# Sparse attention woven into a gated FFN: a half's scores in two units of six PSUM banks instead of three units of four

## The chip, the cores and the metric

The kernel runs on one core of a Trainium2 chip. Times are device microseconds of one execution. The engines are named as the profile names them: PE is TensorE's matmul stream and PEld its weight loads, DVE is VectorE, ACT is ScalarE, POOL is GpSimd, SP is the engine that issues most of the DMAs.

## The reference

Four sequences of 768 positions, 8 heads of 64 channels. Attention is sparse: a query sees the first 8 keys (global) and the last 96 keys up to itself (local), with a bias that falls with distance. The result is the input of a gated FFN of width 1536.

```python
scores = scale * np.matmul(q, k.transpose(0, 1, 3, 2))
keep = is_global | is_local
scores = np.where(keep, scores + bias, -1e9)
a = softmax(scores)
x = np.matmul(a, v)                      # to 3072 tokens x 512
out = (np.maximum(x @ w_gate, 0.0) * (x @ w_val)) @ w_out
```

## The kernel before

**Halves.** The work is cut into 8 halves of a sequence, 384 queries each (s or c = 0 to 7). Halves 0 and 1 form a start of their own. From then on the FFN of half c runs together with the attention of half c+1, in one stream of instructions: `weave` takes the FFN's pieces in order and puts the attention's pieces between them at given fractions of the stage. `spread(items, first, last, n)` gives piece i the fraction first + (i + 0.5)/n x (last - first). The stages with attention in them are c=1 (FFN of halves 0 and 1, attention of half 2) and c=2 to 6 (attention of halves 3 to 7); c=7 is FFN alone. Even c carries the attention of an odd half, odd c that of an even half, and c=3, 5 and 7 also have seven pieces more of the output product.

**FFN pieces.** For each of 12 column blocks a gate product (`gate`, L748, four matmuls of 384 columns), its Relu on ScalarE (L757), a value product (`val`, L748) and its multiply on VectorE (L764). Then the output product in seven pieces (L634, matmuls of 256 columns), in a form with fewer multiplications that needs sums of activations: `Pair.sums`, L627 to L630 on VectorE, four of which are issued after value products 7 to 10. All products take their PSUM bank from a pool of three, `ff_ps` (FFB).

**Attention pieces of a half.** The scores (`score_unit`, L515) of a pair of head pairs pp, key group g and head e of a pair fill one bank: 12 banks in a half. The contraction is 64 rows, so the matmuls of e=0 and e=1 stand in the two halves of TensorE's rows[...]. An even half has groups of 432, 432 and 336 columns, an odd one of 480, 480 and 432. Each bank gets one exponential on ScalarE (`unit_exp`, L524) and one or two mask multiplies on VectorE (`mask`, L536), which carry bias and mask. A mask is not issued with its exponential but with the next one (or with `flush`, which AV calls first). Then for each head pair p: AV products for the two heads (`piece_av`, L431, bank pool `av_ps` of two, AVB), logarithm (L440) and inverse (L446) of the softmax sum on ScalarE, and the normalization (`piece_norm`, N, L453, two multiplies on VectorE), which frees the two AV banks and writes `xT`, the FFN's input.

**Scores before.** There are three units of two groups, so of four banks: one from AVB, three from the score pool `qk_ps` (QKB, three banks). A half's order is

```python
(X(U[0]) + X() + X() + X() + wait + X(U[1]) + X() + X() + a0[0:1] + X() + a0[1:2] + N(0) + wait
 + X(U[2]) + X() + a1[0:1] + X() + X() + a1[1:2] + N(1) + wait * 2 + AV(2) + N(2) + wait * 2
 + AV(3) + [(0.0, lambda: piece_inverse(s, 3))] + N(3))
```

where X(U) is a unit of scores and its first exponential, X() a further exponential with the mask of the one before, a0 and a1 the AV products of p=0 and 1, and `wait` an empty place. Each engine executes its instructions in the order of this stream.

**Beside it.** GpSimd casts the queries and keys of the half after next and puts the keys in order (`early_pieces`: L367, then L278 to L284), in c=2 to 5. In c=1 VectorE also makes eight sums of the output weights (L600).

Of the kernel before, what the change touches and what calls it, by code (L numbers as in the profile page):

```python
# [8 lines left out]
FP32 = mybir.dt.float32  # L9
# [7 lines left out]
def kernel(  # L17
# [12 lines left out]
    nc = tc.nc  # L30
# [8 lines left out]
    HP = H // 2  # L39
    QH = S // 2  # L40
    NN = 3
# [45 lines left out]
    kT = [[const.tile([128, NT, 128], BF16, name=f"kT{i}_{p}") for p in range(HP)] for i in range(2)]  # L87
# [163 lines left out]
    QKB, FFB, AVB = (qk_psum, "qk_ps"), (ff_psum, "ff_ps"), (av_psum, "av_ps")  # L251
# [114 lines left out]
    def piece_cast2(s, p, dst, src):  # L366
        nc.gpsimd.tensor_copy(  # L367
            dst[s % 2].rearrange("t n (h d) -> t h n d", d=D)[:, 2 * p : 2 * p + 2],
            src[s][:, 2 * p : 2 * p + 2, :].rearrange("t e (n d) -> t e n d", n=NN))

    def piece_x(dst, src, n):
        nc.sync.dma_start_transpose(out=dst[:, :, n * 128 : (n + 1) * 128], in_=src[:, n])

    def piece_order(s, p):
        b, half = divmod(s, 2)
        put_keys(nc.gpsimd.tensor_copy, nc.gpsimd.tensor_copy, kT[b % 2][p], kNb[s % 2][:, p], half)

    def early_pieces(s):
        out = [(0.0, lambda p=p: piece_cast2(s, p, kc, ks_of)) for p in range(HP)]
        out += [(0.0, lambda n=n: piece_x(kNb[s % 2], kc[s % 2], n)) for n in range(NN)]  # L380
        out += [(0.0, lambda p=p: piece_cast2(s, p, qc, qs_of)) for p in range(HP)]
        out += [(0.0, lambda n=n: piece_x(qT2[s % 2], qc[s % 2], n)) for n in range(NN)]
        out += [(0.0, lambda p=p: piece_order(s, p)) for p in range(HP)]
        return out
# [35 lines left out]
    def piece_av(s, p, e):  # L420
        b, half = divmod(s, 2)
        h = 2 * p + e
        vb = vbuf[b % 2]
        av = av_psum.tile([128, 512], FP32, name="av_ps")
        av_of[s, p, e] = av
        av3 = av[:, 0:QH].rearrange("d (n p) -> d n p", n=NN)
        todo = [t for bank in banks_of_half[half] for t in bank]
        for i, (j, a, w, m) in enumerate(todo):
            es, c = es_of[s, p, j, e]
            z0 = 2 * D * h + (D if e == 0 else 0)  # L430
            nc.tensor.matmul(av3[:, :, a : a + w],  # L431
                             lhsT=vb[:, j, z0 : z0 + 128],
                             rhs=es[:, c : c + NN * w].rearrange("k (n p) -> k n p", n=NN),
                             start=(i == 0), stop=(i == len(todo) - 1),
                             skip_group_check=True)
        o0, d0 = (0, 64) if e == 0 else (64, 0)
        if e == 0:
            av_of[s, p, "l"] = rc_pool.tile([128, QH], FP32, name="lnd")
        ln = av_of[s, p, "l"]
        nc.scalar.activation(ln[o0 : o0 + 64], av[d0 : d0 + 64, 0:QH], AF.Ln, bias=0.0, scale=1.0)  # L440
        if e == 1 and p < HP - 1:
            piece_inverse(s, p)

    def piece_inverse(s, p):
        rc = rc_pool.tile([128, QH], FP32, name="rcp")
        nc.scalar.activation(rc, av_of[s, p, "l"], AF.Exp, bias=0.0, scale=-1.0)  # L446
        av_of[s, p, "r"] = rc

    def piece_norm(s, p, e):
        if s not in xT_of:  # L450
            xT_of[s] = xt_pool.tile([128, N_DC, QH], BF16, name="xT")
        r = slice(64 * e, 64 * e + 64)
        nc.vector.tensor_tensor(xT_of[s][r, p, :], av_of[s, p, e][r, 0:QH], av_of[s, p, "r"][r],  # L453
                                op=ALU.mult)
# [20 lines left out]
    def piece_norm_wide(s, p):  # L475
        piece_sums_wide(s, p)
        piece_mul_wide(s, p)
# [17 lines left out]
            xT_of[s] = xt_pool.tile([128, N_DC, QH], BF16, name="xT")  # L495
        nc.vector.tensor_tensor(xT_of[s][:, p, :], av_of[s, p][1][:, 0:QH], av_of[s, p, "r"], op=ALU.mult)

    def score_unit(s, groups, pools):


        b, half = divmod(s, 2)
        out = []
        for pp, g in groups:
            banks = []
            for e in range(2):
                pool, name = pools.pop(0)
                banks.append(pool.tile([128, 512], FP32, name=name))
                out.append((pp, g, e, banks[e]))
            c = 0
            for j, a, w, m in banks_of_half[half][g]:  # L510
                for p in (2 * pp, 2 * pp + 1):
                    for e in range(2):
                        r = slice(64 * e, 64 * e + 64)
                        q3 = qT2[s % 2][r, p].rearrange("d (n p) -> d n p", n=NN)
                        nc.tensor.matmul(banks[e][:, c : c + NN * w], lhsT=kT[b % 2][p][r, j, :],  # L515
                                         rhs=q3[:, :, a : a + w], start=True, stop=True)
                    c += NN * w
        return out

    def unit_exp(s, pp, g, e, ps):  # L520
        bank = banks_of_half[s % 2][g]
        cols = sum(2 * NN * w for _, _, w, _ in bank)
        es = es_pool.tile([128, 480], BF16, name="es")
        nc.scalar.activation(es[:, 0:cols], ps[:, 0:cols], AF.Exp, bias=0.0, scale=scale)  # L524

        def mask():
            c = 0
            for j, a, w, m in bank:
                n_ = 2 * NN * w
                e4 = es[:, c : c + n_].rearrange("k (i n p) -> k i n p", i=2, n=NN)  # L530
                h0 = 4 * pp + e
                mk = m_all[:, h0 : h0 + 3 : 2, 0 if j == 0 else 1, :, m : m + w]
                if w == WQ:
                    e4 = e4.rearrange("k i n p -> k i (n p)")
                    mk = mk.rearrange("k i n p -> k i (n p)")
                nc.vector.tensor_mul(e4, e4, mk)  # L536
                for i in range(2):
                    es_of[s, 2 * pp + i, j, e] = (es, c + i * NN * w)
                c += n_

        return mask

    def attention_pieces(s):
        masks, units = [], []

        def flush():
            for f in masks:
                f()
            masks.clear()

        def scores(groups, pools):
            units.extend(score_unit(s, groups, list(pools)))

        def x(scored=None):
            ready = masks[:]
            masks.clear()
            if scored:
                scores(*scored)
            masks.append(unit_exp(s, *units.pop(0)))
            for f in ready:  # L560
                f()

        U = [([(0, 0), (0, 1)], (AVB, QKB, QKB, QKB)),
             ([(0, 2), (1, 0)], (AVB, QKB, QKB, QKB)),
             ([(1, 1), (1, 2)], (AVB, QKB, QKB, QKB))]
        X = lambda u=None: [(0.0, lambda: x(u))]
        AV = lambda p: [(0.0, lambda e=e: (flush(), piece_av(s, p, e))) for e in range(2)]
        N = lambda p: [(0.0, lambda: (piece_norm(s, p, 0), piece_norm(s, p, 1)))]
        wait = [(0.0, lambda: None)]
        a0, a1 = AV(0), AV(1)  # L570

        return (X(U[0]) + X() + X() + X() + wait + X(U[1]) + X() + X() + a0[0:1] + X() + a0[1:2] + N(0) + wait
                + X(U[2]) + X() + a1[0:1] + X() + X() + a1[1:2] + N(1) + wait * 2 + AV(2) + N(2) + wait * 2
                + AV(3) + [(0.0, lambda: piece_inverse(s, 3))] + N(3))


    out_v = out.rearrange("(s p n) d -> s n p d", p=128, n=NN)

# [229 lines left out]
    def spread(items, first, last, n=None):  # L808

        n = n or len(items)  # L810
        return [(first + (i + 0.5) / n * (last - first), f) for i, (_, f) in enumerate(items)]
# [28 lines left out]
    def AV(s, p, *pools):  # L840
        piece_av_wide(s, p, *pools)
        piece_norm_wide(s, p)
# [139 lines left out]
    def T2_piece(p):  # L982
# [9 lines left out]
          spread(T2, 0.55, 0.95))  # L992
    sums_wo = [(0.0, f) for i in (0, 3) for f in weight_sums(i, i + 3)]
    weave(f1_0[G[2]] + f1_1[G[2]] + f2_0 + f2_1,
          spread(attention_pieces(2), 0.02, 0.86, 30), spread(early_pieces(3), 0.1, 0.76),
          spread(sums_wo, 0.08, 0.4))

    for c in range(2, NHALF):
        placed = []
        if c + 1 < NHALF:  # L1000
            placed.append(spread(attention_pieces(c + 1), 0.0, 0.85 if c % 2 else 0.87, 30))
        if c + 2 < NHALF:
            load_qk(c + 2, 0, H)
            load_v_half(c + 2)
            placed.append(spread(early_pieces(c + 2), 0.25, 0.75))
        f1, f2 = ffn_pieces(c)
        weave(f1 + f2, *placed)
# [35 lines left out]
```

The softmax here doesn't subtract the row's maximum and nothing guards it: scores larger than these inputs give would overflow.

## Time and profile before

Three runs: median 238.47 us, from 237.69 to 238.80. The profiled execution has a span of 235.6 us.

| engine | busy us | share of the span | instructions |
|---|---|---|---|
| PE | 228.5 | 97% | 2021 |
| PEld | 157.8 | 67% | 2021 |
| DVE | 187.1 | 79% | 466 |
| ACT | 146.1 | 62% | 321 |
| POOL | 88.4 | 38% | 191 |

Some of the groups, as the list by shape has them:

| group | count | busy us | mean ns |
|---|---|---|---|
| L748, gate and value products, 384 columns | 768 | 77.9 + 77.7 | 326 |
| L764, value multiply (DVE) | 96 | 53.3 | 556 |
| L757, Relu (ACT) | 96 | 46.7 | 489 |
| L524, exponential, 432 columns, from `qk_ps` (ACT) | 27 | 13.7 | 533 |
| L524, exponential, 480 columns, from `qk_ps` (ACT) | 18 | 9.9 | 572 |
| L536, mask, 432 columns (DVE) | 36 | 13.6 | 401 |
| L453, normalization (DVE) | 48 | 26.5 | 553 |

A matmul's duration runs from its start to its end in the pipeline, so two neighbours overlap: what counts for throughput is the distance from start to start, which the timeline shows. The same holds, by less, for ScalarE and VectorE.

### The profile page before, as it was taken

To read this page: it belongs to the slowest core of one execution; us is meant where nothing else is said; L and a number is where in the kernel's file an instruction comes from. 1 tells how busy PE (TensorE), PEld (TensorE's weight loads), DVE (VectorE), ACT (ScalarE), POOL (GpSimd) and SP (SyncE) were. 2 spreads that over 40 slices of the span, in tenths; PEclk is the share of its full clock that TensorE was granted. 3 is DMA by queue.
4 is the path that set the end of the run, shared out by engine and by line. 5 is a ranking of instruction groups with operands and counts; after the bars stand their busy time and mean duration, and the time that the engine had idled before them with its cause. 6 is when DMAs were issued, how large, how long until landed. Compare 5 with 4: busy or idle time off the path is not lost.

```text
span 235.6 us, 5509 instructions
## 1 busy us (share of the span) xinstructions
PE 228.5 (97%) x2021; PEld 157.8 (67%) x2021; DVE 187.1 (79%) x466; ACT 146.1 (62%) x321; POOL 88.4 (38%) x191
## 2 busy tenths in 40 slices
PE   7889999999999999999999999999999999999994
PEld 4675766655778666856688666856679566865683
DVE  6877767779988789786999789886899779773784
ACT  7989865677624887467742887567832687524300
POOL 8998904933492066406480066305320000000000
PEclk9999999999999999999999999999999999999999
DMA  6999999998369854766497854846422200020005
GB/s 183 188 181 183 205 272 272 170 108 267 70 177 154 265 147 93 50 182 199 90 79 122 252 159 90 53 151 223 85 36 89 92 0 3 0 92 0 1 3 178
DMA packets 71419, 30.43 MB, mean 129 GB/s; under 512 B 47744, under 2 KB 70784, under 8 KB 71392
## 3 DMA queue, kind: packets, MB, share of 16 engines
q0 software_dynamic: 34896, 10.27, 38.9%
q1 hardware_dynamic: 36496, 19.82, 29.1%
q8 instruction: 16, 0.26, 0.4%
q14 instruction: 11, 0.09, 0.1%
HBM read 28.38 MB, written 6.29 MB: 147 GB/s over the span
## 4 chain that ended last, share of the span: by engine, by line
PE 79%; POOL 7%; DVE 6%; DMA 4%; issue 1%; POOLq 0%; DVEq 0%
PE ff_ps L748 47%; PE ff_ps L634 20%; PE av_ps L431 6%; DMA wv<-in_moe_w_val_dram 4%; POOL vbuf L154 3%; PE ff_ps L781 2%; PE av_ps L515 2%; DVE ht L764 2%; PE qk_ps L515 2%; DVE wo_sum L600 1%; POOL kc L131 1%; DVE obuf L647 1%; DVE es L536 1%; POOL wg L171 1%; POOL qT L195 1%
## 5 line engine op out<-in xcount | busy, mean ns | idle before, releaser
L757 ACT ACTIVATE grelu<-ff_ps 128x384 bf16<-128x384 f32 x96 | 46.7, 489 | 52.0 <-PE ff_ps L748 38.7
L748 PE MATMUL ff_ps<-xT,wv 128*128 128x384 bf16 x384 | 77.9, 326 | 0.1
L748 PE MATMUL ff_ps<-xT,wg 128*128 128x384 bf16 x384 | 77.7, 326 | 0.0
L764 DVE TENSOR_TENSOR ht<-ff_ps,grelu 128x384 f16<-128x384 f32 x96 | 53.3, 556 | 26.8 <-PE ff_ps L748 22.5
L748 PEld LDWEIGHTS <-wv 128*128 128x128 bf16 x384 | 36.0, 98 | 24.1 <-issue 1.3
L748 PEld LDWEIGHTS <-wg 128*128 128x128 bf16 x384 | 36.4, 98 | 21.2 <-issue 0.5
L647 DVE TENSOR_TENSOR obuf<-ff_ps,obuf 128x512 f32<-128x512 f32 (+1 forms) x46 | 27.6, 603 | 5.3 <-ACT rcp L446 2.2
L367 POOL CAST kc<-ks 128x384 bf16<-128x384 f32 x20 | 10.4, 560 | 54.7 <-DMA ks<-in_k_dram 54.7
L536 DVE TENSOR_TENSOR es<-es,m_all 128x432 bf16<-128x432 bf16 (+3 forms) x108 | 30.4, 325 | 0.2 <-ACT es L524 0.2
L453 DVE TENSOR_TENSOR xT<-av_ps,rcp 64x384 bf16<-64x384 f32 x48 | 26.5, 553 | 5.0 <-ACT rcp L446 4.3
L440 ACT ACTIVATE lnd<-av_ps 64x384 f32<-64x384 f32 x48 | 23.3, 485 | 11.1 <-PE av_ps L431 10.2
L524 ACT ACTIVATE es<-qk_ps 128x432 bf16<-128x432 f32 (+2 forms) x54 | 27.7, 532 | 0.0
L154 POOL DMA_DIRECT2D vbuf<-in_v_dram x29 | 24.7, 861 | 0.3 <-DVE hsum L630 0.3
L431 PEld LDWEIGHTS <-vbuf 128*128 128x128 bf16 x216 | 18.3, 98 | 4.8 <-DVE xT L453 0.4
L431 PE MATMUL av_ps<-es,vbuf 128*128 128x216 bf16 (+4 forms) x216 | 21.4, 226 | 0.0
L634 PEld LDWEIGHTS <-ht 128*128 128x128 f16 x198 | 18.6, 97 | 3.5 <-DVE ht L764 0.5
L634 PEld LDWEIGHTS <-hsum 128*128 128x128 f16 x192 | 18.5, 98 | 2.1
L634 PE MATMUL ff_ps<-wo_sb,ht 128*128 128x256 f16 x132 | 18.5, 272 | 0.2 <-DVE ht L764 0.2
L634 PE MATMUL ff_ps<-wo_sum,hsum 128*128 128x256 f16 x144 | 17.2, 273 | 0.0
L446 ACT ACTIVATE rcp<-lnd 128x384 f32<-128x384 f32 x24 | 12.6, 523 | 0.7
L524 ACT ACTIVATE es<-av_ps 128x432 bf16<-128x432 f32 (+2 forms) x18 | 9.5, 528 | 2.0 <-PE qk_ps L515 2.0
L515 PEld LDWEIGHTS <-kT 64*128 64x128 bf16 x216 | 6.6, 94 | 6.1 <-issue 3.8
(130 smaller groups left out, 263.2 us busy)
## 6 DMA issues: line engine op xcount, KB each, us to landing
out_dram<-obuf SPq DMA_DIRECT2D x22, 256.0 KB
ks<-in_k_dram SPq DMA_DIRECT2D x5, 768.0 KB
qs<-in_q_dram SPq DMA_DIRECT2D x5, 768.0 KB
vbuf<-in_v_dram POOLq DMA_DIRECT2D x23, 120.0 KB, 4.6
wv<-in_moe_w_val_dram POOLq DMA_DIRECT2D x3, 512.0 KB, 9.9
wo_sb<-in_moe_w_out_dram POOLq DMA_DIRECT2D x1, 1536.0 KB, 21.1
wg<-in_moe_w_gate_dram POOLq DMA_DIRECT2D x2, 512.0 KB, 9.9
ks<-in_k_dram SPq DMA_DIRECT2D x4, 192.0 KB
```

What stands on the lines that cost most here:

```text
L154: nc.gpsimd.dma_start(out=v_dst(b, NG + r0, NG + r0 + n, j), in_=v[b, :, KT * j + r0 : KT * j + r0 + n, :].rearrange("h p d -> p h d"))
L431: nc.tensor.matmul(av3[:, :, a : a + w], lhsT=vb[:, j, z0 : z0 + 128], rhs=es[:, c : c + NN * w].rearrange("k (n p) -> k n p", n=NN), star ...
L440: nc.scalar.activation(ln[o0 : o0 + 64], av[d0 : d0 + 64, 0:QH], AF.Ln, bias=0.0, scale=1.0)
L453: nc.vector.tensor_tensor(xT_of[s][r, p, :], av_of[s, p, e][r, 0:QH], av_of[s, p, "r"][r], op=ALU.mult)
L515: nc.tensor.matmul(banks[e][:, c : c + NN * w], lhsT=kT[b % 2][p][r, j, :], rhs=q3[:, :, a : a + w], start=True, stop=True)
L524: nc.scalar.activation(es[:, 0:cols], ps[:, 0:cols], AF.Exp, bias=0.0, scale=scale)
L536: nc.vector.tensor_mul(e4, e4, mk)
L634: nc.tensor.matmul(ps[:, c0 : c0 + DH], lhsT=lhs(i), rhs=rhs(i), start=(i == 0), stop=(i == NP - 1), skip_group_check=True)
L647: add = lambda o, x, y: nc.vector.tensor_tensor(o, x, y, op=ALU.add)
L748: nc.tensor.matmul(st[key][:, 0:QH], lhsT=w_of(w, dc, fc), rhs=xT_of[c][:, dc, :], start=(dc == 0), stop=(dc == N_DC - 1))
L757: nc.scalar.activation(gr, psg[:, 0:QH], AF.Relu, bias=0.0, scale=1.0)
L764: nc.vector.tensor_tensor(ht[:, fc, :], psv[:, 0:QH], st["r", fc], op=ALU.mult)
```

## The change

A half's scores are made in two units, one for each pair of head pairs (pp = 0, 1), of six banks each: for e=0 one bank of the FFN's pool and both AV banks, for e=1 the three of the score pool. Their six exponentials follow each other in six places of the stream. The mask of the sixth gets a place of its own (`flush`), followed by an empty one, and only then come the AV products. With that a half has 35 pieces instead of 31, and `spread` counts 34 places instead of 30. It makes the runs of score matmuls longer and fewer, and gives the last mask time before it is needed; the price is a bank of the FFN's three for the time from the scores to the first exponential.

```diff
-    def score_unit(s, groups, pools):
+    def score_unit(s, pp):
         b, half = divmod(s, 2)
-        out = []
-        for pp, g in groups:
-            banks = []
-            for e in range(2):
-                pool, name = pools.pop(0)
-                banks.append(pool.tile([128, 512], FP32, name=name))
-                out.append((pp, g, e, banks[e]))
+        banks = {}
+        for e, pools in enumerate(((FFB, AVB, AVB), (QKB, QKB, QKB))):
+            for g, (pool, name) in enumerate(pools):
+                banks[e, g] = pool.tile([128, 512], FP32, name=name)
+        for g in range(3):
             c = 0
             for j, a, w, m in banks_of_half[half][g]:
...
-        return out
+        return [(pp, g, e, ps) for (e, g), ps in banks.items()]
...
-        U = [([(0, 0), (0, 1)], (AVB, QKB, QKB, QKB)),
-             ([(0, 2), (1, 0)], (AVB, QKB, QKB, QKB)),
-             ([(1, 1), (1, 2)], (AVB, QKB, QKB, QKB))]
...
-        return (X(U[0]) + X() + X() + X() + wait + X(U[1]) + X() + X() + a0[0:1] + X() + a0[1:2] + N(0) + wait
-                + X(U[2]) + X() + a1[0:1] + X() + X() + a1[1:2] + N(1) + wait * 2 + AV(2) + N(2) + wait * 2
-                + AV(3) + [(0.0, lambda: piece_inverse(s, 3))] + N(3))
+        out = []
+        for pp in range(2):
+            out += X(pp) + X() * 5 + [(0.0, flush)] + wait
+            for p in (2 * pp, 2 * pp + 1):
+                out += AV(p) + ([(0.0, lambda: piece_inverse(s, 3))] if p == HP - 1 else []) + N(p) + wait * 2
+        return out[:-2]
...
-          spread(attention_pieces(2), 0.02, 0.86, 30), spread(early_pieces(3), 0.1, 0.76),
+          spread(attention_pieces(2), 0.02, 0.86, 34), spread(early_pieces(3), 0.1, 0.76),
...
-            placed.append(spread(attention_pieces(c + 1), 0.0, 0.85 if c % 2 else 0.87, 30))
+            placed.append(spread(attention_pieces(c + 1), 0.0, 0.85 if c % 2 else 0.87, 34))
```

The units' exponentials come in the order of the banks: the three of e=0 first, the FFN's bank first of all. The lines after `score_unit` move up by 2 in the changed kernel, those after `attention_pieces` by 7: the mask is L534 there, the exponential L522, the scores L513, the FFN's products L741.

More of the change, by code (lines that the diff above doesn't have):

```diff
@@ L514, in score_unit @@
                         q3 = qT2[s % 2][r, p].rearrange("d (n p) -> d n p", n=NN)
-                        nc.tensor.matmul(banks[e][:, c : c + NN * w], lhsT=kT[b % 2][p][r, j, :],
+                        nc.tensor.matmul(banks[e, g][:, c : c + NN * w], lhsT=kT[b % 2][p][r, j, :],
                                          rhs=q3[:, :, a : a + w], start=True, stop=True)
                     c += NN * w
-        return out
+        return [(pp, g, e, ps) for (e, g), ps in banks.items()]
     def unit_exp(s, pp, g, e, ps):
@@ L549, in flush, with x @@
             masks.clear()
-        def scores(groups, pools):
-            units.extend(score_unit(s, groups, list(pools)))
-        def x(scored=None):
+        def x(pp=None):
             ready = masks[:]
             masks.clear()
-            if scored:
-                scores(*scored)
+            if pp is not None:
+                units.extend(score_unit(s, pp))
             masks.append(unit_exp(s, *units.pop(0)))
@@ L561, in x @@
                 f()
-        U = [([(0, 0), (0, 1)], (AVB, QKB, QKB, QKB)),
-             ([(0, 2), (1, 0)], (AVB, QKB, QKB, QKB)),
-             ([(1, 1), (1, 2)], (AVB, QKB, QKB, QKB))]
-        X = lambda u=None: [(0.0, lambda: x(u))]
+        X = lambda pp=None: [(0.0, lambda: x(pp))]
         AV = lambda p: [(0.0, lambda e=e: (flush(), piece_av(s, p, e))) for e in range(2)]
@@ L569, in attention_pieces @@
         wait = [(0.0, lambda: None)]
-        a0, a1 = AV(0), AV(1)
-        return (X(U[0]) + X() + X() + X() + wait + X(U[1]) + X() + X() + a0[0:1] + X() + a0[1:2] + N(0) + wait
-                + X(U[2]) + X() + a1[0:1] + X() + X() + a1[1:2] + N(1) + wait * 2 + AV(2) + N(2) + wait * 2
-                + AV(3) + [(0.0, lambda: piece_inverse(s, 3))] + N(3))
+        out = []
[4 more added lines that the diff above has]
+        return out[:-2]
     out_v = out.rearrange("(s p n) d -> s n p d", p=128, n=NN)
```

## The prediction

> **What bounds the kernel now.** I read, in this order, the page's busy times and slices, the waits of TensorE, the timeline of one stage, and the groups of instructions by shape.
>
> ```profile
> PE 228.5 (97%) x2021; PEld 157.8 (67%) x2021; DVE 187.1 (79%) x466; ACT 146.1 (62%) x321; POOL 88.4 (38%) x191
> PE av_ps L515 <- DVE xT L453: 0.2, 1, 0.2
> 76.00:100.00 24.00, 24.00 (x217) 16.65 (x216) 19.76 (x52) 17.25 (x37) 10.00 (x23) 1.00 0.65 137
> ```
>
> TensorE is busy for 97% of the span, and for all 24 us of this stage (the gated FFN of half 2, c=2, with the attention of half 3 woven in). The reader sees what that leaves: no large wait to take away. A TensorE instruction less is worth its own time, and a new wait on TensorE costs its full length. VectorE (DVE) is busy for 19.76 of the 24 us, 82%: little room for a burst.
>
> ```profile
> 78.61 0.81 PE L748 MATMUL ff_ps<-xT,wg 128*128 128x384 bf16 x4
> 79.36 0.26 PE L515 MATMUL av_ps<-qT,kT 64*128 64x216 bf16 x1
> ...
> 79.93 0.82 PE L748 MATMUL ff_ps<-xT,wv 128*128 128x384 bf16 x4
> ```
>
> What a score unit costs on TensorE. Gate products start at 77.31, 78.61 and value products at 77.96, so a group of four 384-column products is issued in 0.65 us, 0.42 ns a column. The group at 78.61 is thus issued by 79.26; the unit's first score comes at 79.36 (0.10 us later), and the next product 0.57 us after that. Score matmuls run two side by side (the two 64-row halves), so this unit's 912 columns need 0.39 us: 0.28 of its 0.67 us are not columns. The other two units of the stage (76.12 to 76.65, 85.85 to 86.35) give 0.22 each: mean 0.24. In c=3 the three units take 0.48, 0.46 and 0.45 us, plus 0.10 each, for 2400 columns (1.01 us): mean 0.23.
>
> ```profile
> 58.93 0.26 PE L515 MATMUL av_ps<-qT,kT 64*128 64x216 bf16 x1 [0.15 <-DVE xT L453]
> 172.82 0.28 PE L634 MATMUL ff_ps<-wo_sb,ht 128*128 128x256 f16 x1 [0.20 <-DVE ht L764]
> ```
>
> The only gaps of the woven stages. By issue times they are 0.22 (58.93, beyond the usual 0.10), 0.36 (172.82) and 0.17 us (an AV product at 145.65): 0.75 us. Each is TensorE waiting for a late VectorE.
>
> **What the Trainium skill says.** "TensorEngine Tiling (Array Packing)", Key Properties: changing the tiling mode drains TensorE. The trace agrees: 0.10 us before a unit, about 0.09 after it, not inside it. "PSUM — Partial Sum Buffer", Engine vs sequencer instructions: ScalarE and VectorE queues are strict FIFO, so a mask behind a late multiply is late too; the trace shows them in program order throughout. "SBUF — State Buffer", Who interferes with whom: a VectorE instruction with two SBUF inputs contends with a GpSimd instruction that reads SBUF. The trace agrees: two masks took 1.01 us at 143.13, beside GpSimd's key copies, and 0.67 us at 89.82 without any.
>
> **The change, part by part.**
>
> *One unit less in each half (six halves, 2 to 7).* Matmuls and columns are the same; a pair of mode changes goes. At 0.23 to 0.24 us: 6 x 0.235 = 1.4 us less. If part of that belongs to the short matmuls (24 and 48 columns) and not to the change of mode, only 0.10 + 0.09 is saved: 1.1 us. I take 1.4.
>
> *The old gaps.* The unit that waited at 58.93 for a normalization (L453) is gone; the new second unit comes two to three empty places after N(1). The AV product of 145.65 moves; in odd c the attention no longer crowds the last value product. I count 0.6 of the 0.75 us as removed.
>
> *One FFN bank lent to the unit.* In the changed kernel's order of instructions the value product right after a unit takes the bank of the gate product just before it. In c=2: gate product from 75.38, its Relu (L757) 76.23 to 76.72, six-bank unit from 76.12 for 1392 columns (0.59) plus 0.14: value product at 76.85. The Relu is done 0.1 us before. In odd c: Relu ends 101.27, unit 100.67 + 0.51 + 0.12 = 101.30, a semaphore's 0.05 too late. I put 0.2 us on all twelve units. The exponential of the lent bank comes first of the six, done 1 us before its next user.
>
> *Six exponentials without a gap.* The spacing goes from 0.90 to 0.79 FFN items in even c (31 items x 0.87 over 34 places, not 30). In a row, an exponential of 480 columns takes ScalarE 0.45 us, of 432 0.41, a Relu 0.39: six plus three Relus are 3.8 us. TensorE needs 0.8 + 6 x 0.65 = 4.7 us for the unit and the products meanwhile. ScalarE holds.
>
> *The last mask, and the second unit of even c.* This is where I see the bill. In even c (2, 4, 6) the second unit follows gate product 7, and value products 7 to 10 carry the sums (L627 to L630) as well. Starts that follow without a gap in the trace give VectorE's costs: multiply (L764) 0.48, sum 0.33, masks of an exponential 0.38 (two tiles) or 0.29 (one). Put 0 at the unit's first score. TensorE: v7 0.71, g8 1.36, v8 2.01, g9 2.66, v9 3.31, g10 3.96, v10 4.61, then AV(2) of head 0 at 5.26 and of head 1 at 5.57. VectorE's queue in order: multiply v7 from 1.58 (when v7 has left TensorE), sum, masks 1 and 2, multiply v8, sum, masks 3, 4 and 5, multiply v9, sum: 3 x 0.48 + 3 x 0.33 + 4 x 0.38 + 0.29 = 4.24 us without a pause. So the sixth mask starts at 5.82 and ends at 6.21 (0.39). The last matmul of head 1's AV reads it and would have been issued at 5.82; with 0.05 for the semaphore it goes at 6.26: a wait of 0.45 us. Behind it on TensorE's queue stand gate product 11 and all that follows, so it is lost in full. In c=2 and c=4 GpSimd's key copies (90.22 to 94.06 in c=2) lie beside the end of this queue; bounds 0 and 0.5 us on top, I take 0.25. Sum: 0.45 + 2 x 0.70 = 1.85 us.
>
> *The first unit of even c and both units of odd c.* No sums lie beside the first, and in odd c there is one mask to a product: by the same count the sixth mask is ready 0.3 us or more before its AV product. The added empty place ahead of AV hides it. In the first weave (c=1) eight weight sums (L600) lie beside the masks; I count 0.1 us for a multiply that gives its bank late.
>
> *The rest* is hidden: the order of AV and N changes, their number does not, and the last normalization stays at 0.88 of the stage (34.5/34 x 0.87, before 30.5/30 x 0.87).
>
> Sum: -1.4 - 0.6 + 0.2 + 1.85 + 0.1 = +0.15, which is nothing against a before that spreads from 237.69 to 238.80. I say 238.4 us.
>
> **The rivals.**
> - *VectorE keeps up.* If the sums and masks run a little faster than counted, or a late mask meets a matmul that was late anyway, the 1.85 us shrink to 0.3: 238.47 - 1.4 - 0.6 + 0.3 + 0.3 = 237.1, or with all small items at 0, 236.5. For it: the queue's lateness is only 0.45 us in a chain of 4.24, so an error of 10% clears it. Against: 82% busy on average, and sums and masks in one place.
> - *The burst costs more than the switch saves.* With a bank lent for 1.5 us, a late multiply holds up products too. If each of the five stages c=2 to 6 loses 0.5 us more, and the contention is at its upper bound (2 x 0.25 more): 238.6 + 2.5 + 0.5 = 241.6; half of that, 240.1. For it: the same kind of wait already shows at 58.93 and 172.82. Against: the next user of each multiply's bank in c=2 comes 0.2 us or more after it is free, by the count above.
> - *Only the mode changes count, and no wait changes:* 238.47 - 1.1 = 237.4, between the first two.
>
> **How the numbers follow.** About even 0.47, VectorE keeps up (with the third) 0.34, more waits 0.19. Of the even case (237.5 to 239.5) little lies beyond 0.5% (1.19 us); of the second about four fifths lie under 237.3; of the third four fifths over 239.7. With some of the even case spilling to both sides: faster 0.33, same 0.48, slower 0.19. The range takes in the keep-up case nearly to its end and half of the bad one: 236.4 to 240.4.
>
> **What would show it.** Right: two runs of scores a stage, of some 0.6 us in c=3 and 0.7 in c=2; in c=2, 4 and 6 an idle of 0.4 to 0.8 us on TensorE at the fifth AV product of p=2, head 1 (L431), ended by a mask (now L534), and no gaps like 58.93 and 172.82. Keep-up: no such idle. Bad: idles at FFN products (now L741) ended by a multiply or a Relu. Wrong altogether: units of 0.9 us, or a change larger than 2 us either way.

## The result, and the profile after

The changed kernel takes **241.18 us** (median of 4 executions, 240.64 to 242.20) against 238.43 us for the kernel before, measured beside it (median of 4, 237.69 to 238.80): ratio 1.0124, 95% interval 1.0083 to 1.0166. It is slower by 2.75 us, and outside the predicted range.

The page's busy times of the changed kernel, over a span of 240.3 us (before: 235.6):

```profile
PE 228.9 (95%) x2021; PEld 159.5 (66%) x2021; DVE 186.7 (78%) x466; ACT 145.3 (60%) x321; POOL 90.3 (38%) x191
```

The work is the same: as many matmuls, 0.4 us more of TensorE time. What grew is the time in which TensorE stands still. The stage of c=2, from 77 to 103 us, in the view of busy times by stretch (stretch, its length, then PE, PEld, DVE, ACT and POOL busy, clock, DMA share, GB/s):

```profile
77.00:103.00 26.00, 24.84 (x220) 16.99 (x219) 20.48 (x52) 17.07 (x37) 10.46 (x23) 1.00 0.66 128
```

TensorE filled all 24 us of the stretch shown before; here it is idle for 1.16 of 26 us, at a full clock. The waits of TensorE name the releasers (line waited at, releaser, us in total, times, longest):

```profile
PE av_ps L431 <- DVE es L534: 2.4, 3, 1.0
...
PE av_ps L431 <- DVE xT L453: 0.9, 2, 0.5
...
PE ff_ps L741 <- DVE ht L757: 0.7, 2, 0.5
```

None of the three is among the waits of the kernel before. The first is the predicted one: an AV product that waits for the mask of the sixth exponential, three times. The second was not predicted: AV products that wait for a normalization, twice. The third is a gate product behind a multiply.

To see where the 2.75 us lie, I took the distance from the first score of each stage to the first score of the next, from the start times in TensorE's timeline (us; the last column runs from the first score of c=6 to the start of the last matmul; "woven" is the sum of the columns c=1 to the last):

| kernel | first score | c=1 | c=2 | c=3 | c=4 | c=5 | c=6, 7 | woven |
|---|---|---|---|---|---|---|---|---|
| before | 47.91 | 28.21 | 24.55 | 28.76 | 24.73 | 29.12 | 48.60 | 183.98 |
| after | 48.84 | 28.28 | 25.88 | 29.21 | 26.33 | 29.07 | 48.98 | 187.75 |

The woven stages lose 3.8 us, most of it in c=2 (+1.33) and c=4 (+1.60), some in c=3 (+0.45) and c=6, 7 (+0.38). The other 0.9 us of the spans' difference lie ahead of the first woven score. The two profiled executions are 242.20 and 237.49 us, 4.7 apart, where the medians are 2.75 apart: the profile of after is the slowest of its four executions, that of before is below its median. So the table tells where the time went, not to a tenth of a us how much.

TensorE in c=2, from the product behind the second unit on (start, duration, engine, line, operands, count, and the idle time before with its releaser; durations overlap, so starts are compared):

```profile
88.98 0.82 PE L741 MATMUL ff_ps<-xT,wv 128*128 128x384 bf16 x4
...
91.59 0.81 PE L741 MATMUL ff_ps<-xT,wv 128*128 128x384 bf16 x4
92.58 0.81 PE L741 MATMUL ff_ps<-xT,wg 128*128 128x384 bf16 x4 [0.17 <-DVE ht L757]
...
93.87 0.77 PE L431 MATMUL av_ps<-es,vbuf 128*128 128x72 bf16 x9
95.63 0.25 PE L431 MATMUL av_ps<-es,vbuf 128*128 128x216 bf16 x1 [0.99 <-DVE es L534]
```

Groups of four follow each other every 0.65 us. The one at 92.58 would have started at 92.25: 0.33 us lost. The last matmul of AV(2), head 1, goes 1.15 us later than the nine before it allow, and those nine need 0.59 us from the first start to the ninth, where the same nine in c=6 need 0.49. Together 1.58 us in this stage. VectorE's queue over the same time:

```profile
89.92 0.56 DVE L757 TENSOR_TENSOR ht<-ff_ps,grelu 128x384 f16<-128x384 f32 x1 [0.69 <-PE ff_ps L741]
90.51 0.42 DVE L620 TENSOR_TENSOR hsum<-ht 128x512 f16<-128x512 f16 x1
90.85 1.21 DVE L534 TENSOR_TENSOR es<-es,m_all 128x144 bf16<-128x144 bf16 x4
91.98 0.55 DVE L757 TENSOR_TENSOR ht<-ff_ps,grelu 128x384 f16<-128x384 f32 x1
92.45 0.47 DVE L621 TENSOR_TENSOR hsum<-hsum,ht 128x512 f16<-128x512 f16 x1
92.84 1.56 DVE L534 TENSOR_TENSOR es<-es,m_all 128x432 bf16<-128x432 bf16 x5
94.33 0.54 DVE L757 TENSOR_TENSOR ht<-ff_ps,grelu 128x384 f16<-128x384 f32 x1
94.80 0.46 DVE L622 TENSOR_TENSOR hsum<-ht 128x512 f16<-128x512 f16 x1
95.18 0.40 DVE L534 TENSOR_TENSOR es<-es,m_all 128x432 bf16<-128x432 bf16 x1
```

It is the queue that the prediction wrote out, instruction for instruction, without a pause after 89.92. From the first multiply to the sixth mask it takes 5.26 us; the prediction said 4.24. The masks account for most of the excess: five of them in 1.56 us. Beside them runs GpSimd:

```profile
91.06 0.65 POOL L278 COPY kT<-kN 128x360 bf16<-128x360 bf16 x1 [3.01 <-DMA kN<-kc]
...
94.92 0.43 POOL L280 COPY kT<-kT 128x56 bf16<-128x56 bf16 x1
```

In c=6 there are no key copies, and the same queue takes 4.38 us (200.41 to 204.79). The AV product there:

```profile
204.04 0.68 PE L431 MATMUL av_ps<-es,vbuf 128*128 128x72 bf16 x9
205.21 0.25 PE L431 MATMUL av_ps<-es,vbuf 128*128 128x216 bf16 x1 [0.50 <-DVE es L534]
```

By issue times 0.66 us are lost. In c=4, with copies again, the two places are:

```profile
148.05 0.81 PE L741 MATMUL ff_ps<-xT,wg 128*128 128x384 bf16 x4 [0.54 <-DVE ht L757]
...
151.17 0.25 PE L431 MATMUL av_ps<-es,vbuf 128*128 128x216 bf16 x1 [0.91 <-DVE es L534]
```

By issue times 0.71 us are lost at the gate product, 0.25 among the nine AV matmuls and 1.07 at the tenth: 2.03 us.

The wait that was not predicted, in c=3, TensorE first and then VectorE:

```profile
123.11 2.13 PE L627 MATMUL ff_ps<-wo_sum,hsum 128*128 128x256 f16 x18
125.69 0.42 PE L431 MATMUL av_ps<-es,vbuf 128*128 128x216 bf16 x4 [0.45 <-DVE xT L453]
```

```profile
124.02 0.69 DVE L640 TENSOR_TENSOR obuf<-ff_ps,obuf 128x512 f32<-128x512 f32 x1 [0.29 <-ACT lnd L440]
124.63 0.55 DVE L621 TENSOR_TENSOR qT<-qT,ht 128x768 f16<-128x768 f16 x1
125.10 1.13 DVE L453 TENSOR_TENSOR xT<-av_ps,rcp 64x384 bf16<-64x384 f32 x2
```

AV(3) takes the AV bank that N(2) frees. The order of AV and N and the two empty places between N(2) and AV(3) are those of the kernel before, but a stage now has 34 places and not 30. So N(2) comes one product piece later than before, and AV(3) behind the same piece. On VectorE N(2) now stands behind a result's add (L640) and a sum across the pair (L621, 768 columns). In the kernel before, both came after it (the sum at 123.21):

```profile
121.43 1.14 DVE L453 TENSOR_TENSOR xT<-av_ps,rcp 64x384 bf16<-64x384 f32 x2 [0.31 <-ACT rcp L446]
122.60 0.69 DVE L647 TENSOR_TENSOR obuf<-ff_ps,obuf 128x512 f32<-128x512 f32 x1
```

It isn't ScalarE that holds N(2) in the changed kernel: the inverse that N(2) reads is done at 124.35, 0.75 us before N(2) starts. TensorE could have gone on at 125.07; it goes at 125.69: 0.62 us. c=5 has the same wait with the same 0.62 (181.09).

### The profile page after: what moved, and what is told of

Its sections match the earlier page's. It is cut to its first block, busy times and chain, and to the rows that moved or that the text cites. A ratio compares the mean times of both kernels' runs of the same rounds, so it can differ in the third digit from the quotient of the medians.

```text
span 240.3 us, 5510 instructions
## 1 busy us (share of the span) xinstructions
PE 228.9 (95%) x2021; PEld 159.5 (66%) x2021; DVE 186.7 (78%) x466; ACT 145.3 (60%) x321; POOL 90.3 (38%) x191
## 4 chain that ended last, share of the span: by engine, by line
PE 79%; DVE 8%; POOL 4%; DMA 4%; issue 2%; ACT 1%; POOLq 0%; DVEq 0%
PE ff_ps L741 47%; PE ff_ps L627 18%; PE av_ps L431 5%; DMA kc<-in_q_dram 4%; DVE es L534 2%; DVE ht L757 2%; DVE obuf L640 2%; PE av_ps L513 2%; PE ff_ps L774 1%; POOL vbuf L154 1%; PE ff_ps L513 1%; DVE xT L453 1%; DVE wo_sum L593 1%; POOL kc L131 1%; PE av_ps L468 1%
## 5 line engine op out<-in xcount | busy, mean ns | idle before, releaser
L741 PE MATMUL ff_ps<-xT,wg 128*128 128x384 bf16 x384 | 77.7, 326 | 0.7 <-DVE ht L757 0.7
L741 PE MATMUL ff_ps<-xT,wv 128*128 128x384 bf16 x384 | 77.8, 326 | 0.0
L741 PEld LDWEIGHTS <-wg 128*128 128x128 bf16 x384 | 36.6, 98 | 25.2 <-issue 4.0
L741 PEld LDWEIGHTS <-wv 128*128 128x128 bf16 x384 | 36.2, 98 | 23.7 <-issue 1.3
L640 DVE TENSOR_TENSOR obuf<-ff_ps,obuf 128x512 f32<-128x512 f32 (+1 forms) x46 | 27.6, 603 | 5.7 <-ACT rcp L446 2.2
L534 DVE TENSOR_TENSOR es<-es,m_all 128x432 bf16<-128x432 bf16 (+5 forms) x108 | 30.1, 328 | 0.5 <-ACT es L522 0.4
L627 PE MATMUL ff_ps<-wo_sb,ht 128*128 128x256 f16 x132 | 17.8, 272 | 0.0
L522 ACT ACTIVATE es<-qk_ps 128x432 bf16<-128x432 f32 (+2 forms) x36 | 17.7, 541 | 0.0
L522 ACT ACTIVATE es<-av_ps 128x432 bf16<-128x432 f32 (+2 forms) x24 | 11.9, 525 | 0.0
L367 POOL CAST qc<-qs 128x384 bf16<-128x384 f32 x20 | 9.7, 525 | 1.0 <-DMA qs<-in_q_dram 1.0
```

The source lines that it names most:

```text
L367: nc.gpsimd.tensor_copy(dst[s % 2].rearrange("t n (h d) -> t h n d", d=D)[:, 2 * p : 2 * p + 2], src[s][:, 2 * p : 2 * p + 2, :].rearrange ...
L627: nc.tensor.matmul(ps[:, c0 : c0 + DH], lhsT=lhs(i), rhs=rhs(i), start=(i == 0), stop=(i == NP - 1), skip_group_check=True)
L640: add = lambda o, x, y: nc.vector.tensor_tensor(o, x, y, op=ALU.add)
L741: nc.tensor.matmul(st[key][:, 0:QH], lhsT=w_of(w, dc, fc), rhs=xT_of[c][:, dc, :], start=(dc == 0), stop=(dc == N_DC - 1))
```

## The experiments

Ratios are to the kernel before, measured on the same chip beside each. Runs without a ratio are one profiled execution.

**again: the changed kernel as it is.**

> The changed kernel once more, nothing edited. First score of a stage to first score of the next was 25.9, 29.2, 26.3 and 29.1 us in c=2 to 5, against 24.6, 28.8, 24.7 and 29.1 before, and everything up to the first woven score came 0.9 us later than before. Theory (waits of TensorE for late VectorE work in the woven stages): the stage distances repeat within 0.3 us, the 0.9 us of the start do not. Rival (the change makes the start later): the first woven score is again at 48.8 us and not at 47.9.

242.10 us against 237.72; stages 28.32, 25.88, 29.07, 26.32, 29.35, 48.98, woven 187.93, first score at 48.47. The stage distances repeat within 0.3 us, and to 0.01 in c=2 and c=4. The waits are the schedule's, not a stray of one execution.

**before_again: the kernel before as it is.**

> The kernel before once more, nothing edited. Theory: its woven stages take 184.0 us again within 0.3 us, and its first woven score comes at 47.8 to 48.9 us, as in the profiles of all kernels so far, whatever the kernel, by when the inputs arrive. Rival: it comes at 47.9 again, which would speak for a start that the change makes later.

237.06 us; woven 183.96 (183.98 in the first profile). The first score comes at 47.60. So the difference between the woven stages, 3.8 us in the first profiles and 4.0 in these, stands on two profiles of each kernel.

**order_late: the key copies moved later in even stages.** This was to take them away from the masks.

> The changed kernel, with GpSimd's key copies (L278 to L284) moved from the middle of a stage to 0.86 to 0.98 of it, away from the second unit's masks. Theory of contention (masks and sums slowed by GpSimd's copies make the AV wait of c=2 and 4, 1.5 and 2.0 us, longer than that of c=6, 0.66 us): c=2 and 4 fall to 0.4 to 0.8 us of wait, 1.5 to 2.5 us less in all, about 239 us. Rival (the queue alone is too long, whatever GpSimd does): waits of c=2 and 4 stay over 1.2 us, time 240.5 to 241.5.

```diff
-            placed.append(spread(early_pieces(c + 2), 0.25, 0.75))
+            early = early_pieces(c + 2)
+            placed.append(spread(early[:-HP], 0.25, 0.64))
+            placed.append(spread(early[-HP:], 0.86, 0.98))
```

241.53 us, 1.0157 (1.0139 to 1.0175); woven 187.31. Nothing was tested by it: the copies still ran from 91.79 us on, where they had started at 91.06. They are late in the stream, but nothing that comes ahead of them on GpSimd's queue waits for the stage; the queue runs ahead and stops only at the first copy's transfer. A place in the order of instructions is not a time. Its ratio serves as a second one for a kernel much like the changed one.

**hold_order: the key copies held by a dependency.** In even stages a copy of two columns on GpSimd reads the product of value 10, so the key copies behind it can't start before that.

> The changed kernel, with GpSimd's key copies of c=2 and 4 held until value product 10 is multiplied, by a two-column copy that reads its result (moving the copies in the stream alone did not move them in time, since GpSimd ran ahead). Theory of contention: without the copies beside the masks, c=2 and 4 wait as c=6 does (0.66 us at the last matmul of AV(2), none at the gate product), so the stage distances of c=2 and 4 fall from 25.9 and 26.3 us to 25.1 to 25.3. Rival (the queue is long in any case, and c=6 differs for another reason): they stay over 25.7.

```diff
+    held = const.tile([128, 2], FP16, name="held")
...
-            placed.append(spread(early_pieces(c + 2), 0.25, 0.75))
+            pieces = early_pieces(c + 2)
+            if c % 2:
+                placed.append(spread(pieces, 0.25, 0.75))
+            else:
+                placed.append(spread(pieces[:-HP], 0.25, 0.64))
+                placed.append([(0.85, lambda c=c: nc.gpsimd.tensor_copy(held, ht_of[c][:, 10, 0:2]))])
+                placed.append(spread(pieces[-HP:], 0.86, 0.9))
```

240.38 us, 1.0117 (1.0090 to 1.0143); woven 185.74, with c=2 at 24.97 (25.88) and c=4 at 24.97 (26.33). GpSimd, the masks and the AV product in c=2 (lines are one higher here):

```profile
95.39 0.31 POOL L1004 COPY held<-ht 128x2 f16<-128x2 f16 x1 [5.44 <-DVE ht L758]
95.65 0.53 POOL L279 COPY kT<-kN 128x360 bf16<-128x360 bf16 x1
96.12 0.20 POOL L280 COPY kT<-kN 128x24 bf16<-128x24 bf16 x1
```

```profile
90.11 0.56 DVE L758 TENSOR_TENSOR ht<-ff_ps,grelu 128x384 f16<-128x384 f32 x1 [0.69 <-PE ff_ps L742]
...
91.04 0.86 DVE L535 TENSOR_TENSOR es<-es,m_all 128x144 bf16<-128x144 bf16 x4
...
92.62 1.15 DVE L535 TENSOR_TENSOR es<-es,m_all 128x432 bf16<-128x432 bf16 x5
...
94.49 0.37 DVE L535 TENSOR_TENSOR es<-es,m_all 128x432 bf16<-128x432 bf16 x1
```

```profile
94.91 0.25 PE L432 MATMUL av_ps<-es,vbuf 128*128 128x216 bf16 x1 [0.49 <-DVE es L535]
```

Five masks take 1.15 us instead of 1.56, four 0.86 instead of 1.21, the queue 4.38 instead of 5.26. The gate product's wait is gone, and the AV product loses 0.66 us in c=2, c=4 and c=6 alike, what c=6 lost before. So of the losses of 1.58 and 2.03 us, 0.92 and 1.37 were the copies beside VectorE's queue: shown, and the stage distances fall by as much (0.91 and 1.36). The timed ratios alone would not show it (1.0117 against 1.0124, whose interval is 0.8% wide; against order_late's 1.0157 it is 0.4% less); the stages do.

**sums_late: the sums of the pair moved from value products 7 to 10 to the product pieces after them,** for all stages but the last.

> The changed kernel, with the four sums of activations that were issued after value products 7 to 10 moved behind the product pieces (c=2 to 6), so that they don't stand between the masks of the second unit. Theory (masks and sums in one place of VectorE's queue): the waits at the AV product of c=2, 4, 6 and at the gate product of c=2 and 4 go, 1.33 us of VectorE work out of the queue against waits of 0.66 to 1.95: c=2, 4, 6 lose 0 to 0.4 us each, total 238 to 239.5; the wait of c=3 and 5 at the AV product of p=3 stays or grows, since the sums now stand ahead of N(2). Rival (lent bank): waits at gate and value products stay.

```diff
-            if c > 1 and 7 <= fc < N_FC - 1:
+            if c == NHALF - 1 and 7 <= fc < N_FC - 1:
...
+        early = [] if c == NHALF - 1 else pair.sums(0, 4)
         if c % 2 == 0:
-            return f1, pair.items({"1": late[0:2], "2": late[2:4]}, fresh=True)
+            return f1, pair.items({"1": early[0:2], "2": late[0:2], "4": early[2:4], "6": late[2:4]}, fresh=True)
...
-        return f1, (pair.items({"1": late[0:2], "2": late[2:4], "4": sums[0:1], "6": sums[1:2], "5": sums[2:4]}, fresh=True)
+        at = ({"1": late[0:2], "2": late[2:4], "4": sums[0:1], "6": sums[1:2], "5": sums[2:4]} if c == NHALF - 1 else
+              {"1": early[0:2], "2": late[0:2], "4": early[2:4], "6": late[2:4] + sums[0:1], "5": sums[1:4]})
+        return f1, (pair.items(at, fresh=True)
```

240.07 us, 1.0094 (1.0078 to 1.0111); woven 186.59. The wait for the sixth mask falls to 0.53 us in c=2, and to none in c=4 and c=6, so the sums are the other part of the late mask. But the sums go where N(2) already was late: AV(3)'s wait in c=3 and c=5 grows from 0.62 to 0.90. And the first unit of c=3 and c=5 now starts 0.28 us later than in the changed kernel, because the FFN bank lent to it is freed by a result's add (L640): here lending does cost time. VectorE's work was moved, and the loss with it.

**sums_hold: sums_late and hold_order together.**

> The changed kernel with both edits of sums_late and hold_order: the four sums behind the product pieces, the key copies of c=2 and 4 held. Theory (the late sixth mask of even c is made of the sums ahead of it, 0.66 us, and of GpSimd's copies beside it, 0.8 to 1.3 us): no wait over 0.1 us is left at AV(2) in c=2, 4 and 6. Rival (something else holds the mask): a wait of 0.3 us or more stays in c=2 or 4.

240.79 us (one execution); woven 186.57. The ten matmuls of AV(2) follow each other without a wait in c=2, 4 and 6: sums and copies together account for the late sixth mask. The 0.90 at AV(3) and the late first units stay, so the kernel gains nothing over hold_order.

**n2_place: one empty place more between N(2) and AV(3).**

> The changed kernel, with one empty place more between N(2) and AV(3), 35 places instead of 34. Theory (in c=3 and 5 AV(3) waits 0.62 us for N(2), which stands in VectorE's queue behind sums and a result's addition that waits for TensorE): N(2) comes one product piece, 0.65 us, before where it came; the wait at AV(3) falls to 0 to 0.2 us, c=3 and 5 each 0.4 to 0.6 us shorter. Rival (N(2) waits for ScalarE's logarithm and inverse after AV(2)): the wait moves along and stays over 0.4 us.

```diff
-                out += AV(p) + ([(0.0, lambda: piece_inverse(s, 3))] if p == HP - 1 else []) + N(p) + wait * 2
+                out += AV(p) + ([(0.0, lambda: piece_inverse(s, 3))] if p == HP - 1 else []) + N(p) + wait * (3 if p == 2 else 2)
...
-            placed.append(spread(attention_pieces(c + 1), 0.0, 0.85 if c % 2 else 0.87, 34))
+            placed.append(spread(attention_pieces(c + 1), 0.0, 0.85 if c % 2 else 0.87, 35))
```

238.35 us (20 executions), 1.0042 (1.0024 to 1.0059); woven 183.76, as before's. AV(3) in c=3:

```profile
121.75 1.69 PE L627 MATMUL ff_ps<-wo_sum,hsum 128*128 128x256 f16 x14
123.28 0.42 PE L431 MATMUL av_ps<-es,vbuf 128*128 128x216 bf16 x4
```

No wait there, nor in c=5. The edit did more than it was made for: 35 places in the stage shift each piece a little earlier among the FFN's items. In even stages a value product now comes between the two heads of AV(2), which gives the sixth mask 0.65 us, and on VectorE that mask now stands ahead of the multiply and the sum of value product 9. Its wait is gone in c=2 and c=6. In c=4, with the same order, TensorE still loses 0.20 and 0.63 us at the second head. Both stages have copies beside the masks. VectorE and GpSimd in c=2, then VectorE in c=4:

```profile
92.41 1.15 DVE L534 TENSOR_TENSOR es<-es,m_all 128x144 bf16<-128x144 bf16 x5
```

```profile
92.04 1.59 POOL L279 COPY kT<-kN 128x24 bf16<-128x24 bf16 x1
```

```profile
145.83 1.91 DVE L534 TENSOR_TENSOR es<-es,m_all 128x144 bf16<-128x144 bf16 x5
```

In c=2 the masks kept their 1.15 us and a copy of 24 columns, which takes 0.20 us in hold_order, took 1.59; in c=4 the masks were slowed. Why it goes one way or the other, no run here tells, so one profile of this kernel (the fourth fastest of its 20 executions) need not stand for the others. The two effects of the edit are not separated; what the run shows is that a place or two decides over both waits. In c=1 a new wait of 0.55 comes up, at the first product of the result (59.83), for a multiply behind the weight sums.

**av2_places: two empty places more ahead of AV(2).**

> The changed kernel, with two empty places more ahead of AV(2) and AV(3), 36 places instead of 34. Theory (the last mask is 0.45 to 1.4 us late for AV(2) in even c): AV(2) then stands 0.6 to 1 us later against the masks, so its wait in c=6 goes and in c=2 and 4 falls under 0.6 us each. What it does to N(2) and AV(3) of c=3 and 5 is open; the theory of N(2) behind sums says that the wait there is between 0 and 0.6 us. Total 239 to 240.5 us.

```diff
-            out += X(pp) + X() * 5 + [(0.0, flush)] + wait
+            out += X(pp) + X() * 5 + [(0.0, flush)] + wait * (1 + 2 * pp)
```

(and 36 places in `spread`). 243.18 us, 1.0235 (1.0197 to 1.0273); woven 188.79, the worst of all. No AV product waits for a mask any more. Instead a gate product waits 1.02 us in c=2 (93.09) for a multiply, AV(3) waits 0.3 in odd stages, and one of the result's products 0.58 (120.87). A wait taken away by moving pieces came back elsewhere.

**av_alt: the AV products take the AV bank and a score bank in turn,** so that AV(3) need not wait for N(2).

> The changed kernel, with the AV products of odd p in the score pool's banks instead of AV's own two, so that AV(1) needs no N(0) and AV(3) no N(2); both AV follow each other, then both N, 32 places instead of 34. If the waits at AV(2) and AV(3) are the price of the change and two units its gain (0.25 us a half), then without these waits the kernel takes 1.0 to 2.0 us less than before: woven stages of 182.5 to 183.5 us against 184.0 before and 187.8 changed. If other waits take their place (the second unit then waits for both N), over 184.5.

```diff
-        av = av_psum.tile([128, 512], FP32, name="av_ps")
+        pool, name = (AVB, QKB)[p % 2]
+        av = pool.tile([128, 512], FP32, name=name)
...
+            out += X(pp) + X() * 5 + [(0.0, flush)] + wait * (1 + pp) + AV(2 * pp) + AV(2 * pp + 1) + N(2 * pp)
+            out += ([(0.0, lambda: piece_inverse(s, 3))] if pp else wait) + N(2 * pp + 1) + wait * (1 - pp)
```

(and 32 places). 241.41 us, 1.0163 (1.0139 to 1.0186); woven 186.80. The wait went from AV(3) to the second unit, which now needs both normalizations of the first: 0.37 us in even stages, 0.74 and 0.42 in c=1, and 0.25 to 0.48 at products of the FFN.

**lend: the kernel before, with a bank of the FFN instead of an AV bank in each of its three units.**

> The kernel before, with the first bank of each of its three units taken from the FFN's pool and not from AV's: the lending of a bank alone, three times a half. Theory (lending costs nearly nothing, the lateness of VectorE does): 238.0 to 239.3 us, and idle of TensorE at FFN products under 0.7 us in all. Rival (with two banks left, FFN products wait): 240 us or more, with idles at L748 ended by L757 or L764.

```diff
-        U = [([(0, 0), (0, 1)], (AVB, QKB, QKB, QKB)),
-             ([(0, 2), (1, 0)], (AVB, QKB, QKB, QKB)),
-             ([(1, 1), (1, 2)], (AVB, QKB, QKB, QKB))]
+        U = [([(0, 0), (0, 1)], (FFB, QKB, QKB, QKB)),
+             ([(0, 2), (1, 0)], (FFB, QKB, QKB, QKB)),
+             ([(1, 1), (1, 2)], (FFB, QKB, QKB, QKB))]
```

239.59 us, 1.0069 (1.0049 to 1.0088); woven 186.25. The value product after the first unit of c=2:

```profile
77.39 0.81 PE L748 MATMUL ff_ps<-xT,wv 128*128 128x384 bf16 x4
```

From the unit's first score (76.74) it is 0.65 us to this product, where the kernel before took 0.53: in units of 0.45 to 0.57 us the Relu of the gate product, which holds the bank, is not done in time (76.85 to 77.34 on ScalarE). Against the kernel before, it loses 0.12 to 0.19 us at each unit after a gate product, 0.04 at the first unit of c=3 and c=5, and 1.03 at one product in c=1; the time lies between what the theory and the rival said. In the changed kernel's longer unit (0.72 us in even stages) the value product follows without a gap (88.98 above): the length that the change gives the unit is what hides the lent bank. So lending is no cause of the changed kernel's loss in even stages; in c=3 and c=5 the changed kernel's first unit starts the same 0.04 us late.

**both: n2_place and hold_order together.**

> The changed kernel with both amendments: one empty place more between N(2) and AV(3) (35 places), and GpSimd's key copies of c=2 and 4 held until value product 10. Theory: in even c no wait is left at AV(2) and in odd c none at AV(3), so what is left of the change is one unit less in a half, 0.25 us each: woven stages of 182.7 to 183.5 us against 184.0 before, the time 0.5 to 1.3 us under that of before. Rival (held copies make GpSimd's next transfers late, or N(2) and the first weave's waits grow): woven stages over 184, the time equal or longer.

237.30 us (22 executions, before 237.55 in 43), 1.0004 (0.9990 to 1.0018): as fast as before. First score at 48.42, then 28.61, 24.41, 28.64, 24.41, 28.44, 48.42: woven 182.94, 1.0 us less than before. The timed runs don't show this gain: the profile is the second fastest of the 22 executions, and its first score comes 0.8 us later than that of before_again. So the woven stages came out as expected, and the 0.5 to 1.3 us less in time did not. c=2 at the place where 1.58 us were lost:

```profile
92.25 0.81 PE L742 MATMUL ff_ps<-xT,wg 128*128 128x384 bf16 x4
92.90 0.47 PE L432 MATMUL av_ps<-es,vbuf 128*128 128x72 bf16 x5
93.21 0.81 PE L742 MATMUL ff_ps<-xT,wv 128*128 128x384 bf16 x4
93.86 0.47 PE L432 MATMUL av_ps<-es,vbuf 128*128 128x72 bf16 x5
94.16 0.81 PE L742 MATMUL ff_ps<-xT,wg 128*128 128x384 bf16 x4
```

No idle. Of TensorE's waits for VectorE in the woven stages one is left that matters, 0.68 us by issue times, in c=1:

```profile
60.04 1.46 PE L775 MATMUL ff_ps<-wo_sb,ht 128*128 128x512 f16 x6 [0.51 <-DVE ht L758]
```

**both_wo: both, with the weight sums of c=1 earlier.**

> As both, and the eight weight sums of the first weave earlier (0.02 to 0.34 of the stage, not 0.08 to 0.4), away from the multiplies whose lateness made the product at 59.1 us wait 0.55 us. Theory: that wait falls to 0 to 0.2 us, the time 0.3 to 0.5 us under both. Rival: the sums then make the masks of the first unit late and the wait moves to the AV product of p=0: no gain.

```diff
-          spread(sums_wo, 0.08, 0.4))
+          spread(sums_wo, 0.02, 0.34))
```

237.18 us (22 executions), 0.9981 (0.9966 to 0.9997); woven 182.85, first score at 47.89. The wait in c=1 falls from 0.68 to 0.36, not to the expected 0.2 or less, with a new one of 0.21 at 52.65. The profile is the fastest of the 22 executions. By its ratio this is the fastest kernel measured here, by 0.2%, which is little and near the edge of what can be told.

The stages of the four kernels that matter side by side (us):

| kernel | c=1 | c=2 | c=3 | c=4 | c=5 | c=6, 7 | woven | ratio |
|---|---|---|---|---|---|---|---|---|
| hold_order | 28.52 | 24.97 | 29.09 | 24.97 | 29.21 | 48.98 | 185.74 | 1.0117 |
| n2_place | 28.48 | 24.41 | 28.58 | 25.36 | 28.50 | 48.42 | 183.76 | 1.0042 |
| both | 28.61 | 24.41 | 28.64 | 24.41 | 28.44 | 48.42 | 182.94 | 1.0004 |
| both_wo | 28.34 | 24.41 | 28.64 | 24.41 | 28.63 | 48.42 | 182.85 | 0.9981 |

## Why the prediction was wrong

*One unit less in each half* (-1.4): right. The units and their entries took 1.90 us in an even stage before and take 1.64 now, 1.71 and 1.48 in an odd one: -0.26 and -0.23, about -1.5 over six. The Trainium skill's "TensorEngine Tiling (Array Packing)", Key Properties, has TensorE drain at a change of mode; the traces put a quarter of a us on a pair of them.

*The old gaps* (-0.6): right. The 0.22, 0.17 and 0.36 us are all gone from their places: -0.75. (The 0.17 stood in c=4 in the first profile of before and in c=2 in the second.)

*One bank lent* (+0.2): small, as counted: no value product behind a unit waits, and the first units of c=3 and c=5 lose 0.04 us each. lend shows that shorter units do wait, and sums_late that the lent bank can come late from a result's add.

*Six exponentials without a gap*, and the masks of the other units: right. TensorE waits for neither in the woven stages.

*The last mask, and the second unit of even c* (+1.85): **the step that failed, in its size.** The place, the waiting matmul, the releaser and the queue were as written. The cost is 1.58 + 2.03 + 0.66 = 4.27 us. Two terms of it were too small. Without copies (c=6) the wait is 0.66, not 0.45: the queue takes 4.38 us, not 4.24, and its first multiply starts some 0.07 later (89.92, after a first score at 88.27 in c=2). Most of the 0.14 is in one place: the first sum starts 0.59 us after the multiply whose product it reads, not 0.48, as it did in the kernel before (88.89 to 89.48). With copies the loss is larger by 0.92 and 1.37 us, where I took 0.25 in a range of 0 to 0.5. The bound was drawn from one slow pair of masks, as though it met one or two of the queue's. Nor was its other pair, 0.67 us at 89.82, free of copies: one ran from 90.22 on and took 0.67 us itself, against 0.53 in hold_order. Two masks take the same 0.67 us at 81.33, where GpSimd is idle. So the time without contention was right, but of the two pairs beside copies only one was slowed, which is too little to draw a bound from. In the changed kernel the copies lay beside most of the queue's masks and its sums, and so late a queue also held up the multiply that frees a gate product's bank (0.33 and 0.71). The Trainium skill's "SBUF — State Buffer", Who interferes with whom, names this contention of two SBUF inputs against a GpSimd read, and hold_order agrees: with the copies held back, all three stages lose the same 0.66.

*The first weave* (+0.1): 0.39 us inside the second unit of c=1 (62.60), whose AV bank waits for N(1). A normalization, and not a weight sum's multiply, as the step had it; under *the old gaps* the prediction had taken this unit to be clear of N(1).

*"The rest is hidden: the order of AV and N changes, their number does not"* (0): **failed too.** Not even the order changes, only the places among the FFN's pieces. But in odd stages N(2) slides one product piece nearer to AV(3), and on VectorE behind a result's add and a sum across the pair: 0.62 us each in c=3 and c=5, 1.24 in all. A normalization's cost was counted by its number; what had to be asked was what it queues behind, and who waits.

Put together with the measured terms: -1.5 - 0.75 + 0.1 + 4.27 + 1.24 + 0.39 = +3.75 us, which is the 3.8 between the woven stages of the two profiles within what their gaps vary. In the medians the kernels are 2.75 us apart.

*The rivals.* "The burst costs more than the switch saves" gave 240.1 to 241.6 us and is what happened, by more AV waits than FFN waits. Its argument against, that each bank is free 0.2 us before its next user, failed where the copies made the queue 0.9 us longer. The upper end of the range took half of this case; with contention bounded too low, that was not enough.

*What stays open.* In the profiles the first woven score comes at 47.6 to 47.9 us in the three with the old attention and at 47.85 to 48.84 in the eleven with the new, though in before and after the instructions ahead of it are in the same order on every engine. Waits for the transfers of v, keys and the value weights stand in other places each time. Whether the change has a part in it, or the transfers' times only scatter, no run here tells.

## What to carry to other kernels

A pair of mode switches is worth a quarter of a us here, but a longer burst of exponentials is also a longer burst of masks, so the whole queue of the engine that finishes the burst has to be written out, with the contended duration for every instruction that another engine's copies can reach. Of each piece that moves, its normalizations too, ask what it now queues behind and who waits for it: one empty place decided over 0.6 us. To move work on an engine whose queue runs ahead, give it something to wait for; its place in the stream alone moved the copies by 0.7 us.

## What the runs showed of the hardware

- VectorE's masks with both inputs in SBUF, beside GpSimd's copies: five in 1.56 us against 1.15, four in 1.21 against 0.86; a sum of 512 columns 0.47 against 0.41. GpSimd's copies suffer too: 24 columns took 0.33 us beside masks (91.66), 0.40 beside a sum and a mask (92.59), and 0.20 in hold_order at 96.12. Which side is slowed varies: in n2_place five masks in c=2 kept 1.15 us and a 24-column copy took 1.59, in c=4 five masks took 1.91.
- Without copies beside it, VectorE's queue of eight instruction groups ahead of the sixth mask was foretold from start distances to 0.14 us (4.24 against 4.38): within some 3%.
